# Retention layer and top-2 mixture of experts on one core: the first expert's w1 loaded and cast later, its low products last, other turn halves

## The chip, the cores and the metric

The kernel runs on one core of a Trainium2 chip. The metric is the device time of one execution in microseconds, the median of the runs shown. A profiled execution gives the trace; its span is the time from the first to the last instruction that the profiler saw.

## What is computed

```python
state = zeros(B, H, D, D)                       # B, H, S, D = 4, 8, 768, 64
for t in range(S):
    state = gamma[h] * state + outer(k[:, :, t], v[:, :, t])
    y[:, :, t] = q[:, :, t] @ state / sqrt(D)
x = y as [3072 tokens, 512]
noisy = x @ w_gate + log1p(exp(x @ w_noise)) * noise     # 8 experts
top2, weights = the two largest of noisy, softmax over the two
for e in range(8):                              # w1[e] 512 x 1024, w2[e] 1024 x 512
    out[tokens of e] += weight * (relu(x[tokens of e] @ w1[e]) @ w2[e])
```

All inputs and outputs are float32.

## The kernel before

**First part, the steps.** The tokens are 24 chunks of 128 (4 batches of 6). `step(j)` works on chunk j. On TensorE it issues, in this order: the score products of the next chunk (`qk(j + 1)`, L354), the turn of the chunk before (`x_turn(j - 1)`, L405), the product with the running state (`y_state(j)`, L371, not in the first chunk of a batch), the product of the masked scores with the scaled values (`y_mm(j)`, L378), and the state's update (L388, not in the last chunk of a batch). VectorE masks the scores (`am`, L359) and scales the result (`yt`, L382), GpSimd scales the values (`vp`, L335) and makes the low half of x (`x_low`, L437), ScalarE does squares, splits and copies. x goes to memory as two fp16 halves (`x_store`, L448).

**Turns.** `x_turn` transposes y and multiplies by the gate weights at once. For a chunk in the list `HALVES` it issues 8 matmuls of 128 rows of y; for a chunk that is not in the list 16 matmuls of 64 rows (two parts of the same work). So a turn "in halves" is one whose number is not in the list. The turn of chunk j runs in step j + 1. A float32 matmul shows as two in the trace.

**Inputs.** Each chunk has two loads of 512 KB, `in_qk` and `in_vk`, with AHEAD + 1 = 5 buffers. All are issued by SyncE, which takes its instructions in program order. Before the steps chunks 0 to 3 are issued, then `load(j + 4)` in step j.

**Second part, the experts.** Routing by VectorE tables gives each expert a list of token rows. `gather` reads them (GpSimd's indirect DMA), `x_t` transposes them by DMA into `xe`. Weights come in four parts (`w_load`), are squared and summed for a scale (`w_sum`, L210, `w_scale`), cast to an fp16 high part (`w_hi`, L233) and, by VectorE, to a low part `w1l` (`w_lo_half`, L245, half a part at a time). Each product is three matmuls: high x high, high x low, low x high. The first 384 tokens of expert 0 (`first(0)` to `first(7)`, eight units of 12 matmuls, L888 to L890) start while the last chunks' routing is still being worked out; `step(23)` stands in the middle of `first(0)`.

**What sets the order.** The kernel runs under a manual schedule: every engine's order is that of the code. `at(j, f)`, `at0(j, f)` and `P(j, f)` put work at the end of step j, in the order `late`, `mid` (P), `todo` (at), `first_todo` (at0). `own_a`, `own_h` and `own_t` build the tables of expert 0's tokens (`a` of 128 lanes, `ob` of 7 blocks), `own_m` multiplies them, `slots` makes the row indices; `route_e` copies the running counts (`cum`).

## Time and profile before

| | |
|---|---|
| median of 3 runs | 643.73 us (641.87 to 644.48) |
| the profiled execution's own time | 644.79 us |
| its span | 643.0 us |
| TensorE busy | 625.2 us, 97% |
| ScalarE, VectorE, GpSimd busy | 302.7, 291.1, 203.6 us |
| moved by DMA | 113.04 MB |

The profiled execution took 1.06 us more than the median, and its span leaves out 1.8 us of its own time. A view by line or time gives start, duration, engine, source line and operation (output <- inputs); a bracket tells how long the engine had been idle and what it waited for. The end of a matmul is modelled, so the length of a step is read from the starts of its matmuls.

### The profile page before, as it was taken

Reading aid. Unit: us, or ns where it says so; the run is one execution under the profiler, and the core shown is the slowest. Engines: PE = TensorE matmul, PEld = TensorE weight load, DVE = VectorE, ACT = ScalarE, POOL = GpSimd, SP = SyncE. Lnnn points to the kernel's source line nnn. Section 1 sums busy time; section 2 is a strip of 40 time slices with the busy share of each in tenths; the row PEclk is TensorE's granted clock in tenths of the full one; section 3 lists DMA queues with packets and bytes.
Section 4 is the critical chain, followed back from the end, with each engine's and each line's share of the span. In section 5 each row is a group of like instructions: output and inputs, shape, how many; then the busy total and the mean of one; then the engine's idle time right before and its main releaser. Section 6 shows DMA issues by size and latency. Waiting matters only on the chain.

```text
span 643.0 us, 12833 instructions
## 1 busy us (share of the span) xinstructions
PE 625.2 (97%) x5223; PEld 379.2 (59%) x5223; DVE 291.1 (45%) x736; ACT 302.7 (47%) x582; POOL 203.6 (32%) x169
## 2 busy tenths in 40 slices
PE   8998989999999999999999999999999999999995
PEld 5887877559578545554455445544554465455574
DVE  4667997997454221654262226222622262215020
ACT  5778557615652443554354344434543454344121
POOL 2555556032540143104320533043303420430214
PEclk9999999999999999999999999999999999999998
DMA  8999997998769067736673567557744764472303
GB/s 304 407 407 407 325 368 139 335 243 294 163 106 303 10 123 131 234 84 110 123 212 131 102 130 199 143 88 129 202 151 84 134 197 148 91 140 35 49 9 44
DMA packets 87656, 113.04 MB, mean 176 GB/s; under 512 B 59910, under 2 KB 61068, under 8 KB 84012
## 3 DMA queue, kind: packets, MB, share of 16 engines
q1 hardware_dynamic: 75808, 85.56, 43.4%
q0 software_dynamic: 11776, 26.63, 22.5%
q8 instruction: 42, 0.69, 0.4%
q14 instruction: 18, 0.15, 0.1%
q10 hardware_dynamic: 12, 0.01, 0.0%
HBM read 72.66 MB, written 26.42 MB: 154 GB/s over the span
## 4 chain that ended last, share of the span: by engine, by line
PE 90%; DVE 3%; DMA 2%; issue 2%; POOL 1%; ACT 1%; SPq 0%; POOLq 0%; ACTq 0%; DVEq 0%
PE pH L888 13%; PE pH L890 13%; PE pH L889 13%; PE pO L934 12%; PE pO L936 12%; PE pO L935 12%; PE pY L378 3%; PE pA L354 3%; PE pT L405 2%; PE pT L990 2%; PE pO L978 2%; PE pY L371 1%; DMA xbuf<-x 1%; PE pU L388 1%; DMA in_vk<-vk 1%
## 5 line engine op out<-in xcount | busy, mean ns | idle before, releaser
L925 POOL DMA_INDIRECT out<-ot,idx x51 | 84.4, 1654 | 320.4 <-ACT ot L920 191.7
L888 PE MATMUL pH<-xe,w1h 128*128 128x384 f16 (+5 forms) x576 | 180.9, 314 | 1.1 <-DVE ga L539 1.1
L890 PE MATMUL pH<-xe,w1l 128*128 128x384 f16 (+5 forms) x576 | 180.9, 314 | 0.0
L889 PE MATMUL pH<-xe,w1h 128*128 128x384 f16 (+5 forms) x576 | 180.8, 314 | 0.0
L897 DVE SCALAR_TENSOR_TENSOR hl<-pH,hh 128x384 f16<-128x384 f32 (+5 forms) x144 | 75.6, 527 | 140.1 <-ACT hh L894 139.4
L936 PE MATMUL pO<-w2h,hl 128*128 128x512 f16 x344 | 130.4, 379 | 0.0
L935 PE MATMUL pO<-w2l,hh 128*128 128x512 f16 x344 | 130.4, 379 | 0.0
L934 PE MATMUL pO<-w2h,hh 128*128 128x512 f16 x344 | 130.4, 379 | 0.0
L894 ACT ACTIVATE hh<-pH 128x384 f16<-128x384 f32 (+5 forms) x144 | 67.1, 467 | 122.9 <-PE pH L890 112.0
L920 ACT ACTIVATE ot<-pO,gse 128x512 f32<-128x512 f32 x45 | 30.9, 687 | 155.2 <-PE pO L936 142.9
L238 DVE SCALAR_TENSOR_TENSOR w1l<-wst,wsc,w1h 128x1024 f16<-128x1024 f32 x28 | 35.9, 1283 | 97.6 <-ACT w1h L233 97.6
L888 PEld LDWEIGHTS <-w1h 128*128 128x128 f16 x576 | 56.3, 98 | 34.2 <-issue 3.9
L890 PEld LDWEIGHTS <-w1l 128*128 128x128 f16 x576 | 56.3, 98 | 31.0
L889 PEld LDWEIGHTS <-w1h 128*128 128x128 f16 x576 | 56.3, 98 | 29.7
L210 ACT ACTIVATE junk<-wst 128x1024 bf16<-128x1024 f32 x64 | 67.2, 1050 | 0.0
L743 POOL DMA_INDIRECT xg<-xbuf,idx x54 | 55.3, 1025 | 29.3 <-issue 12.4
L936 PEld LDWEIGHTS <-hl 128*128 128x128 f16 x344 | 33.6, 98 | 40.6
L934 PEld LDWEIGHTS <-hh 128*128 128x128 f16 x344 | 33.6, 98 | 40.6 <-issue 0.4
L935 PEld LDWEIGHTS <-hh 128*128 128x128 f16 x344 | 33.6, 98 | 39.6
L437 POOL TENSOR_TENSOR x<-x,x 128x512 f16<-128x512 f32 x23 | 27.4, 1190 | 41.2 <-ACT x L436 19.3
L233 ACT ACTIVATE w2h<-wst,wsc 128x1024 f16<-128x1024 f32 x32 | 36.5, 1139 | 0.8 <-DVE wsc L188 0.8
L233 ACT ACTIVATE w1h<-wst,wsc 128x1024 f16<-128x1024 f32 x32 | 36.2, 1137 | 0.0
(185 smaller groups left out, 660.0 us busy)
## 6 DMA issues: line engine op xcount, KB each, us to landing
wst<-w SPq DMA_DIRECT2D x28, 1024.0 KB, 7.8
in_qk<-qk SPq DMA_DIRECT2D x24, 512.0 KB, 7.9
in_vk<-vk SPq DMA_DIRECT2D x23, 512.0 KB, 8.7
xbuf<-x SPq DMA_DIRECT2D x24, 256.0 KB, 7.2
out<-zero SPq DMA_DIRECT2D x6, 1024.0 KB, 8.8
wst<-w SPq DMA_DIRECT2D x8, 512.0 KB, 7.4
xg<-xbuf,idx POOLq DMA_INDIRECT x54, 4.7
xe<-xg SPq DMA_TRANSPOSE x54, 4.5
```

What stands on the lines that cost most here:

```text
L210: nc.scalar.activation(junk, st[:, i * 1024:(i + 1) * 1024], AF.Square, accum_out=ss[:, i:i + 1])
L233: nc.scalar.activation(hi, st[:, i * 1024:(i + 1) * 1024], AF.Copy, scale=sc[:, 0:1])
L743: nc.gpsimd.indirect_dma_start(out=x[:n], out_offset=None, in_=xbuf[:128 + B0 * S] if e == 0 and t < 3 else xbuf, in_offset=bass.IndirectO ...
L888: nc.tensor.matmul(p[:, :n], whi, xh, start=(k == 0), stop=False)
L889: nc.tensor.matmul(p[:, :n], whi, xl, start=False, stop=False)
L890: nc.tensor.matmul(p[:, :n], wlo, xh, start=False, stop=(k == KT - 1))
L894: nc.scalar.activation(hh[:, f, n0:n1], p, AF.Relu)
L897: nc.vector.scalar_tensor_tensor(hl[:, f, n0:n1], p, 0.0, hh[:, f, n0:n1], op0=OP.max, op1=OP.subtract)
L925: nc.gpsimd.indirect_dma_start(out=out, out_offset=bass.IndirectOffsetOnAxis(ap=idx[:n, i:i + 1], axis=0), in_=ot[:n], in_offset=None, com ...
L934: nc.tensor.matmul(p, a, WT["2h"][:, f, :], start=(f == 0), stop=False)
L935: nc.tensor.matmul(p, a, WT["2l"][:, f, :], start=False, stop=False)
L936: nc.tensor.matmul(p, c, WT["2h"][:, f, :], start=False, stop=(f == FT - 1))
```

## The change

The loads of w1's four parts for expert 0 move from steps 2 to 5 to steps 5, 7, 9 and 11, their sums to steps 8, 10, 11 and 13, the casts from steps 9 to 12 to steps 14 to 17. w2's loads move from steps 14 to 17 to 16 to 19, its sums from 18, 20, 22 to 20, 22, 23. Seven of the eight low halves of w1 stood in steps (10, 11, 12, 14, 18, 21, 23); four stand there now (17, 21 and two in 23), and the four others between the units of the first tokens. In those units the four low x high matmuls come after the eight others. Inputs are issued three chunks ahead up to step 13, then four; chunks 0 and 1 come in two DMAs for each load. The list of unhalved turns goes from 11 entries (0 to 14 even, 18, 20, 22) to 8. `own_t` goes ahead of `own_h`, all of `own_h` into step 16, `route_e` into step 17; the last routing's `route_p` and `own_m` move about one unit back.

```diff
-HALVES = [*range(0, 16, 2), 18, 20, 22]
+HALVES = [7, 9, 11, 13, 15, 18, 20, 22]
+MORE = 14
...
+    APART = 2
...
-            if n == "vk" and j == 0:
+            if j < APART:
                 for i in range(2):
                     nc.sync.dma_start(t[:, i], src[:, i * DM:(i + 1) * DM])
...
-    for j in range(3, AHEAD):
-        load(j, ("qk",))
-        load(j - 1, ("vk",))
-    load(AHEAD - 1, ("vk",))
+    load(2, ("vk",))
+    todo_in = list(range(3, NCH))
...
-    P(15, own_h, 0, 0, 2)
     at(16, gates_out, 0)
-    P(16, own_h, 0, 2, 12)
     P(16, own_t, 0)
-    P(16, route_e, 0)
+    P(16, own_h, 0, 0, 12)
...
+    P(17, route_e, 0)
...
-        at(2 + i, w_load, 0, "1", i)
+        at((5, 7, 9, 11)[i], w_load, 0, "1", i)
...
-    for i, j in ((0, 10), (2, 11), (4, 12), (6, 14), (1, 18), (3, 21), (5, 23)):
+    for i, j in ((0, 17), (2, 21), (4, 23), (6, 23)):
         P(j, w_lo_half, 0, "1", i)
...
-        if j + AHEAD < NCH:
-            load(j + AHEAD)
+        while todo_in and todo_in[0] <= j + AHEAD - (j < MORE):
+            load(todo_in.pop(0))
...
+        early = e == 0 and n0 == 0
...
-            nc.tensor.matmul(p[:, :n], wlo, xh, start=False, stop=(k == KT - 1))
+            if not early:
+                nc.tensor.matmul(p[:, :n], wlo, xh, start=False, stop=(k == KT - 1))
+        for k in range(KT if early else 0):
+            nc.tensor.matmul(p[:, :n], WT["1l"][:, k, f * 128:(f + 1) * 128], XE[e][:, k, n0:n1], start=False, stop=(k == KT - 1))
...
+    w_lo_half(0, "1", 1)
...
+    w_lo_half(0, "1", 3)
+    h_lo(*p0)
+    w_lo_half(0, "1", 5)
     w_hi(0, "2", 1)
-    h_lo(*p0)
+    p3 = first(3)
```

**SyncE's queue from step 2 on.** `in_qk` and `in_vk` are a chunk's loads, `xbuf<-x` the store of a finished chunk, `wst` a part of w1, `ct` and `nz` constants and noise. Before:

```order
L448 DMA xbuf<-x_305 128x512
L206 DMA wst_389<-w 128x1024
L272 DMA in_qk<-qk 128x1024
L272 DMA in_vk<-vk 128x1024
L448 DMA xbuf<-x_386 128x512
L206 DMA wst_389<-w 128x1024
L870 DMA nz<-noise 128x192
L272 DMA in_qk<-qk 128x1024
L272 DMA in_vk<-vk 128x1024
L448 DMA xbuf<-x_458 128x512
L206 DMA wst_389<-w 128x1024
L870 DMA ct<-ctab 128x433
```

After:

```order
L449 DMA xbuf<-x_312 128x512
L870 DMA ct<-ctab 128x433
L275 DMA in_qk<-qk 128x1024
L275 DMA in_vk<-vk 128x1024
L449 DMA xbuf<-x_393 128x512
L870 DMA nz<-noise 128x192
L275 DMA in_qk<-qk 128x1024
L275 DMA in_vk<-vk 128x1024
L449 DMA xbuf<-x_470 128x512
L275 DMA in_qk<-qk 128x1024
L275 DMA in_vk<-vk 128x1024
L449 DMA xbuf<-x_552 128x512
```

The four parts of w1 are gone from these steps, and a chunk's loads stand behind the store of a chunk that is one later than before.

**VectorE in steps 16 to 18.** From the tables (`a`, `ob`) of step 16 to the masks `am`; before:

```order
L585 TENSOR_TENSOR a_12_1408<-lanes,lf_12_1406 128x1280
L593 TENSOR_TENSOR ob_12_1493<-blks,lf_12_1406 128x84
L595 TENSOR_TENSOR ob_12_1493<-ob_12_1493,tokn 128x84
L566 COPY cum<-pR 128x9
L567 TENSOR_SCALAR cum<-cum 128x1
L359 TENSOR_TENSOR am<-pA,mask 128x512 x2
L425 TENSOR_SCALAR p2m<-xss 128x1
L426 TENSOR_SCALAR xsa<-p2m 128x1
```

After:

```order
L383 TENSOR_TENSOR yt<-pY,gq 128x512
L594 TENSOR_TENSOR ob_12_1507<-blks,lf_12_1430 128x84
L596 TENSOR_TENSOR ob_12_1507<-ob_12_1507,tokn 128x84
L586 TENSOR_TENSOR a_12_1432<-lanes,lf_12_1430 128x1536
L360 TENSOR_TENSOR am<-pA,mask 128x512 x2
L426 TENSOR_SCALAR p2m<-xss 128x1
```

`ob` is made ahead of `a`, `a` is made in one piece, and the copies to `cum` are gone from in front of the masks. Then the end of step 17, where `idx` is the list of rows for the gather; before, with a low half in step 18:

```order
L656 SCALAR_TENSOR_TENSOR idx<-roww 128x3
L359 TENSOR_TENSOR am<-pA,mask 128x512 x2
L425 TENSOR_SCALAR p2m<-xss 128x1
L426 TENSOR_SCALAR xsa<-p2m 128x1
L382 TENSOR_TENSOR yt<-pY,gq 128x512
L245 SCALAR_TENSOR_TENSOR w1l<-wst_389,wsc_391,w1h 128x512
```

After:

```order
L656 SCALAR_TENSOR_TENSOR roww<-acc 128x3
L657 SCALAR_TENSOR_TENSOR idx<-roww 128x3
L567 COPY cum<-pR 128x9
L568 TENSOR_SCALAR cum<-cum 128x1
L246 SCALAR_TENSOR_TENSOR w1l<-wst_623,wsc_625,w1h 128x512
L360 TENSOR_TENSOR am<-pA,mask 128x512 x2
```

The copies to `cum` and a low half `w1l` now stand between the list and the masks.

**TensorE in the first unit of the expert, behind step 23.** `pH` is the unit's sum, `xe` the gathered tokens. Before, from the end of `y_mm(23)` on:

```order
L378 MATMUL pY<-am,vp 64x128 x8
L888 LDWEIGHTS w1h
L888 MATMUL pH<-xe,w1h 128x384
L889 LDWEIGHTS w1h
L889 MATMUL pH<-xe,w1h 128x384
L890 LDWEIGHTS w1l
L890 MATMUL pH<-xe,w1l 128x384
L888 LDWEIGHTS w1h
L888 MATMUL pH<-xe,w1h 128x384
L889 LDWEIGHTS w1h
L889 MATMUL pH<-xe,w1h 128x384
L890 LDWEIGHTS w1l
```

After, the last rows of the same unit:

```order
L889 LDWEIGHTS w1h
L889 MATMUL pH<-xe,w1h 128x384
L890 LDWEIGHTS w1h
L890 MATMUL pH<-xe,w1h 128x384
L894 LDWEIGHTS w1l
L894 MATMUL pH<-xe,w1l 128x384
L894 LDWEIGHTS w1l
L894 MATMUL pH<-xe,w1l 128x384
L894 LDWEIGHTS w1l
L894 MATMUL pH<-xe,w1l 128x384
L894 LDWEIGHTS w1l
L894 MATMUL pH<-xe,w1l 128x384
```

All four matmuls with `w1l` stand at the end, behind `y_mm(23)`; two of them stood ahead of step 23.

## Rows read from the trace of the kernel before

**Rows 1.** The page: engines' busy us (share) x instructions; instruction queue (packets, MB).

```profile
PE 625.2 (97%) x5223; PEld 379.2 (59%) x5223; DVE 291.1 (45%) x736; ACT 302.7 (47%) x582; POOL 203.6 (32%) x169
...
q8 instruction: 42, 0.69, 0.4%
```

**Rows 2.** Stretches: engines' busy us (x instructions), TensorE's granted clock, DMA share, GB/s.

```profile
4.00:6.00 2.00, 1.94 (x19) 1.08 (x18) 0.42 (x3) 2.00 (x8) 0.00 (x0) 1.00 0.85 180
...
28.00:65.00 37.00, 34.71 (x711) 30.40 (x709) 25.91 (x79) 28.71 (x68) 19.88 (x18) 1.00 1.03 405
...
143.00:643.00 500.00, 492.88 (x2991) 277.01 (x2986) 181.45 (x384) 216.69 (x373) 140.19 (x103) 1.00 0.58 132
```

**Rows 3.** Instructions in order of time: the start, first steps, first "issue" wait.

```profile
2.87 0.91 SPq L270 DMA_DIRECT2D in_vk<-vk  x2
...
8.32 1.16 PE L354 MATMUL pA<-in_qk 64*128 64x128 f32 x16 [1.65 <-DMA in_qk<-qk]
...
10.14 1.09 PE L378 MATMUL pY<-am,vp 128*64 128x128 f32 x16 [0.66 <-POOL vp L335]
...
11.63 1.16 PE L354 MATMUL pA<-in_qk 64*128 64x128 f32 x16
...
15.66 1.16 PE L354 MATMUL pA<-in_qk 64*128 64x128 f32 x16
...
18.29 0.33 SPq L448 DMA_DIRECT2D xbuf<-x  x1
...
19.39 1.16 PE L354 MATMUL pA<-in_qk 64*128 64x128 f32 x16
...
30.08 0.43 PE L371 MATMUL pY<-in_qk,U 64*64 64x128 f32 x2 [0.32 <-issue]
```

**Rows 4.** TensorE's waits, 20 to 107 us: total us, times, longest.

```profile
PE pY L371 <- issue: 2.0, 3, 1.1
...
PE pT L405 <- issue: 1.1, 1, 1.1
```

**Rows 5.** DMA from 9 to 65 us: instruction queue (packets, MB, share); issues with us to landing.

```profile
q8 instruction: 8, 0.13, 1.0%
...
in_qk<-qk SPq DMA_DIRECT2D x15, 512.0 KB, 8.1
```

**Rows 6.** In order of time, steps 16 to 18, and the same `ob` later with GpSimd idle.

```profile
77.31 1.75 PE L354 MATMUL pA<-in_qk 64*128 64x128 f32 x16
...
80.02 1.19 DVE L593 TENSOR_TENSOR ob<-blks,lf 128x84 f16<-128x84 f16 x1
...
83.13 1.75 PE L354 MATMUL pA<-in_qk 64*128 64x128 f32 x16
...
124.07 0.23 DVE L593 TENSOR_TENSOR ob<-blks,lf 128x84 f16<-128x84 f16 x1
```

**Rows 7.** In order of time, steps 18 to 22: a low half beside GpSimd, and TensorE's waits.

```profile
87.29 3.39 DVE L245 SCALAR_TENSOR_TENSOR w1l<-wst,wsc,w1h 128x512 f16<-128x512 f32 x1
...
92.05 1.75 PE L354 MATMUL pA<-in_qk 64*128 64x128 f32 x16 [0.93 <-DVE am L359]
...
94.92 0.78 PE L405 MATMUL pT<-turn,yt 64*64 64x80 f32 x32 [1.11 <-ACT x L431]
```

**Rows 8.** In order of time, the first units of the expert around step 23.

```profile
106.73 0.32 PE L888 MATMUL pH<-xe,w1h 128*128 128x384 f16 x1 [1.07 <-DVE ga L539]
...
110.48 0.34 PE L888 MATMUL pH<-xe,w1h 128*128 128x384 f16 x1
...
111.21 0.74 DVE L245 SCALAR_TENSOR_TENSOR w1l<-wst,wsc,w1h 128x512 f16<-128x512 f32 x1
...
111.56 0.78 PE L405 MATMUL pT<-turn,yt 64*64 64x80 f32 x32
...
111.61 1.35 POOL L437 TENSOR_TENSOR x<-x,x 128x512 f16<-128x512 f32 x1 [2.63 <-ACT x L436]
...
117.79 0.18 PE L512 MATMUL pR<-mb,trib 128*128 128x54 bf16 x1 [0.44 <-DVE mb L501]
```

More of the change, by code (lines that the diff above doesn't have):

```diff
@@ L1047, in moe_kernel @@
     h_hi(*p2)
-    p3 = first(3, lambda: route_p(2))
     route_c(2)
+    w_lo_half(0, "1", 3)
+    h_lo(*p0)
+    w_lo_half(0, "1", 5)
     w_hi(0, "2", 1)
-    h_lo(*p0)
+    p3 = first(3)
     w_lo_half(0, "1", 7)
@@ L1056, in moe_kernel @@
     w_hi(0, "2", 2)
+    p4 = first(4, lambda: route_p(2))
     route_n(2)
+    h_lo(*p3)
     route_d(2)
-    h_lo(*p3)
+    own_a("12")
     route_g(2)
@@ L1063, in moe_kernel @@
         zero_out(i)
-    own_a("12")
-    p4 = first(4)
     h_hi(*p4)
@@ L1070, in moe_kernel @@
     own_t("12")
-    w_lo_half(0, "2", 0)
     p5 = first(5)
@@ L1075, in moe_kernel @@
     h_lo(*p5)
-    w_lo_half(0, "2", 1)
+    w_lo_half(0, "2", 0)
     p6 = first(6)
     h_hi(*p6)
-    own_m("12", 0, NC)
     h_lo(*p6)
+    w_lo_half(0, "2", 1)
     flush()
     out_scale(0, 0, 3)
-    p7 = first(7, lambda: own_m("12", NC, 2 * NC))
+    p7 = first(7, lambda: own_m("12", 0, NC))
+    own_m("12", NC, 2 * NC)
     own_s("12")
```

20 lines of the change are left out of this document (10 added, 10 removed).

## The prediction

> **What bounds the kernel now.** I read the page first, then the stretches, then TensorE's and SyncE's instructions in order of time. TensorE is busy 625.2 of 643.0 us [rows 1]. From 143 us on it works 492.88 of 500 us, and nothing in the diff touches that part [rows 2]; I take it as unchanged. TensorE's clock is granted at 1.00, its 2.4 GHz level, in every stretch, so the clock is no term. What can move is the first 127 us: 24 steps and the first eight units of expert 0. There TensorE is both the longest engine and the one that waits. From 28 to 65 us DMA is at its limit: share 1.03, 405 GB/s [rows 2].
>
> A step's length is read from the starts of its score products. The step from 11.63 to 15.66, with a turn of eight matmuls, took 4.03 us; the next, to 19.39, with the turn in halves, took 3.73 [rows 3]. So the halved turn is the faster one, by 0.30 us, although it has twice the matmuls. The mean is 3.88 us. Many steps are longer, and the reader is to see three kinds of excess: TensorE waits for nothing that the profile names ("issue", four waits of together 3.1 us, the longest 1.1) [rows 4]; it waits on VectorE [rows 6, 7]; it waits at the start, for the first inputs [rows 3].
>
> The "issue" waits I read as waits for instructions. The page has 42 packets of 16 KB on the instruction queue and 10,446 instructions of TensorE, matmuls and weight loads [rows 1], so about one packet for 250 instructions. From 9 to 65 us eight of them passed, in a DMA system that was full [rows 5]. That is an inference from counts.
>
> **The change part by part.** Start: TensorE idles 1.65 us for chunk 1's `in_qk` and 0.66 for chunk 0's scaled values [rows 3], 2.31 in all, which is the most that splitting these loads can give. From 4 to 6 us DMA moved only 180 GB/s at a share of 0.85 [rows 2], so room is there. Against it, two more issues stand ahead of the values' load, and two issues took 0.91 us [rows 3]: a loss of 0.9 at worst. I take the middle, **+0.7**. The Trainium skill's DMA: Bandwidth & Descriptors, section Bandwidth, says to batch transfers to 1 MiB or more, which speaks against the split. No row here compares the two sizes under the same load; by that rule the term would be the loss of 0.9, and the sum 1.6 us worse.
>
> Turns: three fewer entries in the list, three more turns in halves, 3 x 0.30 = **+0.9**. In steps 1 to 7 it is four turns, 1.2 us earlier; 0.3 is given back by step 16. Bounds 0, if inputs or instructions set the pace, and 1.2.
>
> Waits for instructions: before, three parts of w1 were queued by step 4, ahead of chunk 9's load. They go to steps 5 to 11, so the queue is lighter in steps 2 to 4, and as full as before in 5 to 13. I expect half of the 3.1 us back, **+1.5**; above 3.1 nothing is to be had, below see the second rival.
>
> Steps 16 to 18: `ob` took 1.19 us where the same operation takes 0.23 later with GpSimd idle [rows 6]. It ran into GpSimd's work. In the new order it comes ahead of the long `a`, and the `cum` copies leave, so the masks of step 17 can start up to 2 us earlier (two such operations, 0.96 each). TensorE's step from 77.31 to 83.13 took 5.82 us, 2.1 over a halved one; up to 1.1 of it is an "issue" wait, counted above, and the score products after it took 1.75 instead of 1.16 [rows 3, 6]. So 1.0 + 0.6 = 1.6 at most, 0 if `ob` is held again. I take **+1.2**.
>
> Steps 18 to 20: the low half at 87.29 took 3.39 us [rows 7], another 0.74 [rows 8]. Its 2.65 us came out again on TensorE: 0.93 idle, 0.59 in the longer score products, 1.11 on ScalarE, together 2.63 [rows 7]. This half leaves step 18, but one now stands at the end of step 17, ahead of the masks, and GpSimd's subtraction and gather follow there. Even odds that it is held: half, **+1.3**, between 0 and 2.6. For the other halves that leave the steps I count nothing: VectorE is busy 25.9 of 37 us from 28 to 65 [rows 2], and the masks have room.
>
> First unit: TensorE waits 1.07 us at 106.73 [rows 8]. The wait is put down to VectorE's `ga`; the unit also needs the transposed tokens, the end of a chain from step 17's list through gathers and DMA. If that chain starts earlier, it may go. I take half, **+0.5**, between 0 and 1.07.
>
> Low products last: before, `x_turn(23)` stood at 111.56, behind six matmuls from 110.48 on, 0.18 each [rows 8]. Now eight stand there and two fewer ahead of step 23. But two low halves are made by VectorE behind `yt` of step 23. Before, the low half there began at 111.21; the next VectorE work can follow after about 0.65 (estimated from its 0.74, as a start overlaps the end before). Two end at 111.21 + 2 x 0.65 = 112.51, 2.03 after 110.48, plus one matmul 2.21; against 1.08 before, less the 0.36 that left the front: TensorE loses 0.77. GpSimd's subtraction of 1.35 us lies there too [rows 8]; if it holds the second half, the loss is 2.1; I add a quarter of 1.35. Later, `route_p` comes a unit later, so the 0.44 us at 117.79 goes. Together **-0.7**, between -2.1 and -0.3. Three more low halves, 0.74 each, go to VectorE between the units; the later `route_p` and `own_m` cover them with one unit of 12 matmuls, 2.2 us. Without that cover up to 2.2 us would be lost at `own_m`.
>
> ScalarE's casts and sums are the same work in later steps. It is busy 28.7 of 37 us from 28 to 65 [rows 2], and that idle time hides them; without it a cast or sum before the turn's squares would cost its own time of about a us. GpSimd's order is unchanged. Inputs three ahead: a load now stands behind a store, priced as a rival.
>
> Sum: 0.7 + 0.9 + 1.5 + 1.2 + 1.3 + 0.5 - 0.7 = 5.4 us. Against the profiled execution's 644.79 us that is 639.4; it was 1.06 us above the median of 643.73, against which it is 638.3. I take 639.0, between them.
>
> **The rivals.**
>
> *Inputs come late: slower.* Chunk 6's load stands behind chunk 0's store, which came 2.63 us into step 2 (18.29 after 15.66) [rows 3]. Its products are due at the start of step 5, three steps of 3.88 after the start of step 2: 9.0 us remain. A load landed after 8.1 us in the full queue [rows 5]. Each us over 9.0 costs a third of a us in each of the 11 steps for chunks 6 to 16. At 11 us that is 7.3, and the 1.5 on instructions is lost too: 647.8 us. It decides from 9.0 on. Against it: the queue should be shorter, since loads enter later and w1 is spread. Chance 0.08.
>
> *Instructions set the pace of halved turns: no change.* A halved step has 192 instructions of TensorE (96 matmuls, 96 weight loads), the other 160; at 250 a packet that is one packet in 4.9 us instead of 5.5 for alternating steps. Steps 1 to 7 now run seven halved turns in a row, some five packets. At 1.06 us each, the size of the worst waits, 5.3 us are lost and the 1.5 not gained: 645.8. For it: steps 2 and 4 had halves and DMA was as full as later. Against it: the first of the four waits came at 30 us [rows 3], not earlier. Chance 0.12.
>
> *VectorE and GpSimd collide again:* the terms of steps 16 to 18, 18 to 20 and the first unit, 3.0 us, are nothing: 642.0. An operation that is held once is held elsewhere once all shifts. Chance 0.18.
>
> *The "issue" waits have nothing to do with DMA:* 1.5 us are not gained, 640.5. The Trainium skill's Runtime: NRT & Kernel Launch, section Instruction fetch mechanics, says that code is refilled in 16 KiB blocks of 256 instructions and that this is mostly hidden. The packet size agrees with the rows; "hidden" would leave the waits of 1.1 us unexplained. Chance 0.10.
>
> **How the numbers follow.** The forecast, 636 to 641, has 0.52. A measurement of this kernel can tell about 0.5%, 3.2 us, from no change: faster is below 640.5. Faster takes the forecast, half of the last rival and a fifth of the collisions: 0.61. Slower, above 646.9, takes the late inputs and a little of the second rival: 0.10. The rest, 0.29, is no change. The range 635.0 to 644.0 leaves out late inputs, most of the second rival and a better start than I dare to count, together about 0.2.
>
> **What would show it.** Right: steps 1 to 7 at 3.73 us; fewer "issue" waits before 40 us; `ob` near 0.25 us; score products at the start of steps 18 and 20 at 1.16. A wait of about a us on `w1l` in the first unit. Wrong: waits of TensorE for `in_qk` in steps 5 to 15; "issue" waits in steps 2 to 7; a low half of 2 to 3 us at step 17 or 23; a wait at `own_m`.

## The result, and the profile after

The changed kernel took **651.04 us**, the median of four runs (649.42 to 654.51), against 642.8 for the kernel before in the same session: ratio **1.0133**, 95% interval 1.0084 to 1.0182. The forecast was 639.0. It is slower, by more than any case that I priced. All ratios here set the executions of a kernel against those of the kernel before on the same chip; they are close to the quotient of the mean times, and not that of the medians (651.04 to 642.8 would be 1.0128). One execution, of 650.94 us in the last run on the changed kernel, counts as a slow one and is left out of its ratio.

The page of the changed kernel, engines and instruction queue as in [rows 1]:

```profile
PE 627.0 (97%) x5271; PEld 380.7 (59%) x5271; DVE 287.8 (44%) x735; ACT 303.5 (47%) x582; POOL 204.7 (32%) x169
...
q8 instruction: 42, 0.69, 0.4%
```

Its stretches, with the columns of [rows 2]:

```profile
9.00:28.00 19.00, 17.73 (x414) 16.14 (x416) 11.33 (x30) 10.67 (x31) 9.61 (x9) 0.91 0.91 334
28.00:65.00 37.00, 33.44 (x762) 29.95 (x758) 24.42 (x74) 24.82 (x63) 19.46 (x18) 1.00 1.00 378
12.00:14.00 2.00, 2.00 (x20) 1.79 (x16) 0.18 (x1) 0.38 (x1) 1.12 (x2) 0.50 1.01 410
110.00:112.00 2.00, 2.00 (x31) 1.52 (x28) 0.31 (x2) 0.80 (x3) 0.34 (x2) 0.58 0.23 25
```

From 28 to 65 us TensorE is busy 33.44 us, where it was 34.71 [rows 2]. DMA moves 378 GB/s instead of 405, and from 9 to 28 us 334 instead of 412 (the kernel before, same view); eight other profiles with the moved loads, below, have 367 to 385 there, so part of the 334 is this execution's. The two short stretches show what the kernel before did not have before its end: a granted clock of 0.50 and 0.58, the 1.2 GHz level or a mix of both. The page's slices hide it (9 of 10 nearly everywhere); it has to be asked for.

TensorE's waits, 20 to 107 us (as [rows 4]), then 107 to 135:

```profile
PE pY L379 <- issue: 3.1, 2, 1.6
PE pA L355 <- issue: 1.7, 2, 1.3
...
PE pR L515 <- issue: 0.6, 1, 0.6
...
PE pH L889 <- DVE ga L540: 1.6, 1, 1.6
PE pH L889 <- DVE hl L901: 1.0, 1, 1.0
PE pH L894 <- DVE w1l L246: 0.7, 2, 0.4
```

The waits for nothing named are 6.2 us in all from 20 to 107 us, against 3.19 in the kernel before (the 3.1 of [rows 4] and one of 0.18). The order of time tells where they and the low clock lie. All rows are of TensorE, but for one each of VectorE, GpSimd and SyncE:

```profile
10.27 1.09 PE L379 MATMUL pY<-am,vp 128*64 128x128 f32 x16 [1.93 <-POOL vp L336]
...
12.08 2.08 PE L355 MATMUL pA<-in_qk 64*128 64x128 f32 x16
...
35.77 0.44 PE L379 MATMUL pY<-am,vp 128*64 128x128 f32 x4 [1.62 <-issue]
...
42.55 0.60 PE L355 MATMUL pA<-in_qk 64*128 64x128 f32 x5 [1.29 <-issue]
...
79.56 1.34 PE L355 MATMUL pA<-in_qk 64*128 64x128 f32 x16
...
80.40 0.27 DVE L594 TENSOR_TENSOR ob<-blks,lf 128x84 f16<-128x84 f16 x1
...
94.62 0.98 POOL L744 DMA_INDIRECT xg<-xbuf,idx  x1
...
96.04 1.16 PE L355 MATMUL pA<-in_qk 64*128 64x128 f32 x16
...
103.48 2.67 SPq L762 DMA_TRANSPOSE xe<-xg  x1
...
106.03 0.49 PE L379 MATMUL pY<-am,vp 128*64 128x128 f32 x5 [1.53 <-issue]
...
108.73 0.32 PE L889 MATMUL pH<-xe,w1h 128*128 128x384 f16 x1 [1.64 <-DVE ga L540]
...
110.67 1.13 PE L372 MATMUL pY<-in_qk,U 64*64 64x128 f32 x16
111.73 1.97 PE L379 MATMUL pY<-am,vp 128*64 128x128 f32 x16
...
123.94 0.32 PE L889 MATMUL pH<-xe,w1h 128*128 128x384 f16 x1 [1.05 <-DVE hl L901]
```

Read against [rows 3, 6, 7, 8]. Step 1 starts 0.45 us later (12.08), and its score products take 2.08 instead of 1.16, at the low clock behind a wait of 1.93. Two waits of 1.62 and 1.29 us come in steps 6 and 8, in the row of seven halved turns (steps 1 to 7) and right behind it. Step 17 starts 2.25 us late (79.56). Then the forecast gains do come: `ob` takes 0.27 instead of 1.19, and step 21 starts at 96.04, 1.5 us *earlier* than before (97.56 in the trace of before). Then they are lost: the first unit starts at 108.73, 2.0 later than 106.73; the products with the state and with the values behind it take 1.13 and 1.97 us, at the low clock, where the same ones took 0.67 and 1.09 before; the fifth unit waits 1.05 for `hl`, the low half of the hidden values. The second expert product starts 5.1 us late (132.43 against 127.31), the end is 5.7 us late.

### The profile page after: what moved, and what is told of

It reads as the page before. It is cut to its first block, busy times and chain, and to the rows that moved or that the text cites. A ratio compares the mean times of both kernels' runs of the same rounds, so it can differ in the third digit from the quotient of the medians.

```text
span 648.7 us, 12928 instructions
## 1 busy us (share of the span) xinstructions
PE 627.0 (97%) x5271; PEld 380.7 (59%) x5271; DVE 287.8 (44%) x735; ACT 303.5 (47%) x582; POOL 204.7 (32%) x169
## 4 chain that ended last, share of the span: by engine, by line
PE 87%; DVE 7%; DMA 2%; issue 2%; POOL 1%; SPq 1%; ACT 0%; POOLq 0%; DVEq 0%; ACTq 0%
PE pH L889 13%; PE pH L890 12%; PE pH L892 12%; PE pO L938 11%; PE pO L939 11%; PE pO L940 11%; PE pA L355 3%; PE pY L379 3%; PE pT L406 3%; PE pT L994 2%; PE pY L372 1%; DMA in_qk<-qk 1%; PE pU L389 1%; DMA in_vk<-vk 1%; DVE w2l L246 1%
## 5 line engine op out<-in xcount | busy, mean ns | idle before, releaser
L892 PE MATMUL pH<-xe,w1l 128*128 128x400 f16 (+5 forms) x544 | 170.4, 313 | 0.0
L892 PEld LDWEIGHTS <-w1l 128*128 128x128 f16 x544 | 53.2, 98 | 28.9
```

What stands on the lines that cost most here:

```text
L892: nc.tensor.matmul(p[:, :n], wlo, xh, start=False, stop=(k == KT - 1))
```

## Theories

Each experiment below says which of these it tests.

- **T1**: a step with a halved turn has more instructions (192 against 160 of TensorE), and their refills don't keep pace. The new list costs time.
- **T2**: the loss is the work behind step 22: late `w1l`, late `hl`.
- **T3**: the split start costs: late values, a wait, a low clock.
- **T4**, formed after the first four runs: the first unit waits for the gathered tokens, whatever TensorE won in the steps, and the wait is followed by a low clock.
- **T5**: the moved loads cost by themselves. **T7** supposes how: they keep the DMA queues full when the tokens are gathered and transposed.
- **T6**: some of the rows that I took gains from are those of one execution.

In the table "waits" are those of TensorE for nothing named, 9 to 100 us; "tokens" is the time from the third gather's row to the first unit's first product; "ahead" the wait in front of that product; "clock" the sum over stretches of 2 us, from 2 to 140, of 2 us times what the granted clock lacks of 1. One profile each.

| kernel | ratio, interval | waits | tokens | ahead | clock |
|---|---|---|---|---|---|
| before | | 3.19 | 9.6 | 1.07 | 0 |
| before, second profile | | 4.69 | 8.9 | 0.30 | 0 |
| before, no halves | 1.0020, 1.0005 to 1.0035 | 0 | 9.3 | 0 | 0 |
| before, new list | 1.0091, 1.0066 to 1.0117 | 5.30 | 10.4 | 1.81 | 0 |
| before, split start | 1.0028, 1.0016 to 1.0040 | 5.86 | 10.6 | 1.12 | 1.7 |
| before, loads moved | 1.0100, 1.0077 to 1.0123 | 3.48 | 12.1 | 1.49 | 1.7 |
| before, tail | 1.0036, 1.0015 to 1.0057 | 3.33 | 10.3 | 0.56 | 0 |
| before, steps 16 to 18 | 1.0007, 0.9987 to 1.0026 | 2.38 | 11.9 | 1.75 | 0 |
| changed | 1.0133, 1.0084 to 1.0182 | 4.77 | 14.1 | 1.64 | 3.4 |
| changed, old list | 1.0104, 1.0081 to 1.0127 | 3.81 | 13.2 | 4.15 | 3.4 |
| changed, no halves | 1.0087, 1.0059 to 1.0115 | 1.50 | 14.8 | 4.49 | 3.4 |

## Experiments on the changed kernel

**Old list of halved turns.** (The expectation has the parity the wrong way round: steps 2, 4, 6 ... are halved.)

```diff
-HALVES = [7, 9, 11, 13, 15, 18, 20, 22]
+HALVES = [*range(0, 16, 2), 18, 20, 22]
```

> The changed kernel with the old list of halved turns (steps 1, 3, 5, ... halved up to 16); all else as changed. Theory T1 (the refills of TensorE's instructions do not keep pace with the run of halved turns, so two waits of 1.62 and 1.29 us came in steps 6 and 8): the waits for nothing named in steps 6 to 8 go or shrink below 1 us in sum, the score products of step 9 start 1.5 to 3 us earlier than the changed kernel's 46.02, and the whole is 1.5 to 3 us shorter than the changed kernel, ratio to the kernel before about 1.008 to 1.011. Theory T2 (the loss sits behind step 22: late transposes, lower clock, low halves late): step 9 at 45 to 46 and the first unit's first product at the changed kernel's 108.7 or at most 1 us earlier; end within 1 us of the changed kernel. Theory T3 (the split of the first loads): no change either.

Measured 649.06 us, 1.0104. Step 9 starts at 42.09, not 46.02. Of these 3.9 us 2.3 lie ahead of step 2 (14.70 against 17.01), where the profiled execution of the changed kernel had its wait and low clock and this one had neither; from step 2 to step 9 it took 27.4 us against 29.0, which is 1.6 us for T1. But the first unit, in order of time, and two later products:

```profile
106.01 0.48 PE L889 MATMUL pH<-xe,w1h 128*128 128x384 f16 x1 [4.15 <-issue]
...
109.31 1.13 PE L372 MATMUL pY<-in_qk,U 64*64 64x128 f32 x16
110.37 1.97 PE L379 MATMUL pY<-am,vp 128*64 128x128 f32 x16
```

Step 22 starts 3.3 us earlier than in the changed kernel (97.78), the first unit only 2.7, after a wait of 4.15 us, and the clock is at 0.51, 0.50, 0.50 and 0.78 in the stretches from 106 to 114. The span ends 1.3 us earlier: most of what the steps won is gone there, in the wait and the clock behind it. That gave T4. The profile names nothing for this wait; in the next run the same place reads 3.14 us "DMA xe<-xg", the transposed tokens. What ties it to the tokens is the order of time: in all 14 profiles with no other work put ahead of the first unit, its first product comes 2.5 to 4.1 us behind the end of the third transpose's issue, whatever the wait is put down to.

**Start as before**: only chunk 0's `in_vk` is split.

```diff
-            if j < APART:
+            if n == "vk" and j == 0:
```

> The changed kernel with only chunk 0's vk load in two parts, as before; all else as changed. T3 (two more issues ahead of the values' load make vp late, TensorE idles 1.93 us at 10 us and then runs at a granted clock of 0.5 for the score products of step 1): the idle time at 10 us falls to about 0.7, the clock stays at 1.00 between 10 and 16 us, the score products of step 1 take 1.16 instead of 2.08, step 2 starts at about 15.7 instead of 17.01, and the whole is 1 to 1.4 us shorter, if later waits don't eat it. T1 and T2: steps 2 to 5 start earlier, but step 9 or the first unit start where they did within 0.5 us, since another wait takes the place.

Measured 654.69 us, 1.0170 (1.0142 to 1.0197). The start looks as expected: step 2 at 15.10 instead of 17.01, no low clock before 66 us. But the next run keeps the split and has step 2 at 15.17, and none of the other profiles with the split start has a low clock there; so the late start belongs to the one profiled execution of the changed kernel. The time is no better: waits of 1.58 at 66.3, 3.45 at 107.3 and 3.14 at 111.5 go with 6.8 us of lost clock. T3 is not shown, neither for the start nor for the loss.

**w2's loads back in steps 14 to 17.**

```diff
-        at(16 + i, w_load, 0, "2", i)
+        at(14 + i, w_load, 0, "2", i)
```

> The changed kernel with the four loads of w2 back in steps 14 to 17 (changed: 16 to 19); all else as changed. T2 (these loads stand beside the gathered tokens' transposes, whose issues took 2.7 to 3.2 us instead of 1.2 to 1.7, so the first unit starts late and the clock falls to 0.57 behind the wait): the issues of the transposes go back to 1.2 to 1.8 us, the wait of 1.64 us ahead of the first unit's first product falls below 0.7, the clock stays at 1.00 from 108 to 116 us, and the whole is 2 to 3 us shorter than the changed kernel. T1: the transposes' issue may change, but the first unit starts at 108 to 108.7 and the whole is within 1 us of the changed kernel. If the transposes stay as slow, the w2 loads are not their cause.

Measured 652.40 us, 1.0140. The transposes took 1.63, 1.23 and 2.00 us to issue, nearly as expected, and yet the third stood at 103.39, as in the changed kernel (103.48), the clock fell to 0.50 from 108 us on, and the tokens took 13.9 us. T2 in this form is refuted: w2's loads alone are not what makes the tokens late.

**Filler ahead of the first unit**, with the old list: twelve matmuls whose result is not used.

```diff
+    busy(12)
     p0 = first(0, lambda: step(j))
```

> The changed kernel with the old list of halved turns, and twelve matmuls of 128x512 on constants (result unused) between the last products of step 22 and the first unit. New theory T4: steps 16 to 22 did get faster, but the first unit waits for the gathered tokens, whose third transpose does not come earlier with TensorE; the wait of 4.15 us there (without the fill) is followed by 8 us at a granted clock of 0.5, which costs 4.4 us more. T4 expects: the first unit's first product stays at 106.0 us within 1 us, the clock stays at 1.00 from 106 to 114 us, the products from 109 to 112.3 take 0.67 and 1.09 us instead of 1.13 and 1.97, and the whole is 3 to 4.4 us shorter than without the fill, ratio 1.003 to 1.006. Rival T1 (instructions of TensorE come late): 24 more instructions make it later, and the clock has nothing to do with the wait: the same ratio as without the fill, 1.010, or above.

In order of time:

```profile
105.31 2.79 PE L126 MATMUL pA<-const-bfloat16-1.0 128*128 128x512 bf16 x11
108.97 0.32 PE L889 MATMUL pH<-xe,w1h 128*128 128x384 f16 x1 [0.86 <-issue]
...
110.76 0.67 PE L372 MATMUL pY<-in_qk,U 64*64 64x128 f32 x16
111.36 1.09 PE L379 MATMUL pY<-am,vp 128*64 128x128 f32 x16
```

The clock stays at 1.00, and the products take 0.67 and 1.09 as forecast. But 648.61 us, 1.0093, is a miss: 3 to 4.4 us were expected, and by the ratios 0.7 came. From the first unit to the end of the span it gained 2.1 us (539.3 against 541.4), less than the 3.4 of clock, since products that come sooner wait 1.6 us for `w1l` (0.3 without the filler). And this execution came to the first unit 3.0 us later than 106.01, with 6.5 us of waits before 100 us against 3.8, although the two programs are alike up to there.

**Work instead of filler**: the turn and the products of the last chunks ahead of all of the first unit's products, with the old list.

```diff
-            if k == 2 and between:
+            if k == (0 if e == f == 0 else 2) and between:
```

> The changed kernel with the old list of halved turns, and the turn and the products of chunks 22 and 23 (3.7 us of work at full clock) ahead of all of the first unit's products instead of behind the first four. T4: this work fills the wait of 4.15 us, the first unit starts 0 to 1.5 us behind it without a fall of the clock, and the turn of chunk 23 starts at 108 to 109.5 instead of 114.76; whole 5 to 6 us shorter than without it, ratio 1.000 to 1.003. T2 (low halves and the wait for hl set the rest): the same start, but at least 2 us are waited out again behind it for w1l or hl: ratio 1.004 to 1.007. T1: the wait named for nothing moves to the first unit as it stands, ratio near 1.010.

Measured 645.55 us, 1.0045 (1.0025 to 1.0064): 3.5 us less than with the old list alone (3.8 by the ratios), in the range set for T2, short of the 5 to 6 us set for T4. No low clock, and waits of 0.89 for VectorE and 0.43 for ScalarE ahead of the unit; then 1.13 for `w1l` and 1.04 for `hl`.

**No turn in halves.**

```diff
-HALVES = [7, 9, 11, 13, 15, 18, 20, 22]
+HALVES = list(range(NCH))
```

> The changed kernel with no turn in halves. T1 (the seven halved turns in a row outrun the refills of TensorE's instructions): the waits for nothing named before 100 us, 4.8 us in the changed kernel, go as they went in the kernel before without halves; the whole is 3 to 5 us shorter than the changed kernel, ratio 1.005 to 1.008. Rival T5 (the moved loads and casts cost most by themselves, whatever the turns): at most 2 us shorter, ratio 1.010 or above. Either way what is left above 1.000 is to be found behind step 16.

Measured 648.84 us, 1.0087, between the two expectations. Before 98 us waits of 0.55 and 0.15 are left (T1); one of 0.80 stands at 98.87, at a routing product, and the two next kernels without halves have one of 1.36 and 1.55 there, so not every wait for nothing named goes with the halves. GpSimd's third gather, SyncE's third transpose and TensorE's first product, in order of time:

```profile
90.31 0.98 POOL L744 DMA_INDIRECT xg<-xbuf,idx  x1 [0.15 <-issue]
...
98.64 2.42 SPq L762 DMA_TRANSPOSE xe<-xg  x1
...
105.15 0.48 PE L889 MATMUL pH<-xe,w1h 128*128 128x384 f16 x1 [4.49 <-issue]
```

The third gather and the third transpose of the kernel before:

```profile
97.10 0.98 POOL L743 DMA_INDIRECT xg<-xbuf,idx  x1
...
102.08 1.23 SPq L761 DMA_TRANSPOSE xe<-xg  x1
```

The gather starts 6.8 us earlier than in the kernel before, the first unit 1.6 earlier than 106.73 (and 1.0 later than in the second profile of before). The tokens took 14.8 us from there, 9.6 in the kernel before.

**No halves, and the work ahead of the first unit.**

```diff
-HALVES = [7, 9, 11, 13, 15, 18, 20, 22]
+HALVES = list(range(NCH))
...
-            if k == 2 and between:
+            if k == (0 if e == f == 0 else 2) and between:
```

> The changed kernel with no turn in halves, and the turn and products of the last two chunks ahead of all of the first unit's products. Without the second edit TensorE waited 4.49 us ahead of the first unit, and then ran 8 us at a clock of about 0.5 (4.4 us). T7 (the loads that were moved to a later time keep DMA full when the gathered tokens are due, so these come about 4 us later after their gathers than in the kernel before; wait and clock are what is lost): 3.7 us of work fill the wait, the clock stays at 1.00, the turn of chunk 23 starts at 107.5 to 109, the whole is 5 to 6.5 us shorter than without the edit, ratio 0.999 to 1.002. Rival T2 (low halves and the wait for hl lose the rest): at most 4 us shorter, ratio 1.003 or above.

```profile
101.73 1.12 PE L406 MATMUL pT<-turn,yt 64*128 64x80 f32 x16 [0.43 <-ACT x L432]
...
105.70 0.34 PE L889 MATMUL pH<-xe,w1h 128*128 128x384 f16 x1 [1.23 <-DMA xe<-xg]
...
107.76 1.12 PE L406 MATMUL pT<-turn,yt 64*128 64x80 f32 x16
```

**642.11 us, 0.9991 (0.9979 to 1.0004)**: 6.7 us less by the medians, 6.2 by the ratios, as T7 expected (5 to 6.5). The wait left, 1.23 us, is now put down to the transposed tokens, the clock stays at 1.00, and the turn of chunk 23 starts at 107.76. By the ratios the halves are worth 0.5% (with intervals that overlap) and the wait ahead of the first unit with its clock 1.0%; the two edits together take all of the loss away. The clock is not that of one profile: the mean granted clock over the whole span is on record for each execution, 0.996 to 0.998 in all twelve here, 0.988 to 0.995 in the six without the second edit and in the four of the changed kernel. `hl` still costs 1.02 there.

**No halves, and the loads of the kernel before**, four chunks ahead.

```diff
-MORE = 14
+MORE = 0
...
-        at((5, 7, 9, 11)[i], w_load, 0, "1", i)
-        at0((8, 10, 11, 13)[i], w_sum, 0, "1", i)
-        at0(14 + i, w_hi, 0, "1", i)
-        at(16 + i, w_load, 0, "2", i)
+        at(2 + i, w_load, 0, "1", i)
+        at0(5 + i, w_sum, 0, "1", i)
+        at0(9 + i, w_hi, 0, "1", i)
+        at(14 + i, w_load, 0, "2", i)
...
-    for i, j in ((0, 17), (2, 21), (4, 23), (6, 23)):
+    for i, j in ((0, 10), (2, 11), (4, 12), (6, 14)):
```

> The changed kernel with no turn in halves, and w1, w2 and the inputs loaded and cast in the steps of the kernel before, four chunks ahead throughout; the four low halves in steps 10 to 14. The split start, steps 16 to 18, and the part behind step 22 stay as changed. T7: DMA moves 400 GB/s or more from 9 to 65 us again, against 384 to 389; the third gather to the first unit takes 9 to 12 us instead of 14.8, the wait ahead of the first unit falls below 1.8 us, the clock stays at 1.00, the whole is 4 to 5.5 us shorter than with the moved loads, ratio 1.000 to 1.003. Rival (the first unit comes late by the split start or by the tail): the wait stays above 3 us, and the ratio at 1.006 or more.

The same three places as in the kernel without halves:

```profile
90.96 0.98 POOL L746 DMA_INDIRECT xg<-xbuf,idx  x1
...
97.70 1.79 SPq L764 DMA_TRANSPOSE xe<-xg  x1
...
102.09 0.32 PE L891 MATMUL pH<-xe,w1h 128*128 128x384 f16 x1
```

The profile goes as T7 says: tokens in 11.1 us, no wait ahead of the unit, clock at 1.00, DMA at 408 and 407 GB/s from 9 to 65 us. The time does so only in some executions: the twelve lie between 641.25 and 650.94, median 646.41, ratio 1.0041 (1.0015 to 1.0068), 2.4 us less than without the edit (3.0 by the ratios), where 4 to 5.5 were expected. The profiled one took 641.99. The longer ones lose clock: the mean granted clock is 0.998 in the four shortest (up to 643.47) and 0.991 to 0.993 in the six from 645.54 to 648.36, and 0.007 of 645 us is 4.5 us, most of the difference. Behind which wait it falls there was not seen.

## Experiments on the kernel before

**The new list alone.**

```diff
-HALVES = [*range(0, 16, 2), 18, 20, 22]
+HALVES = [7, 9, 11, 13, 15, 18, 20, 22]
```

> The kernel before with the new list of halved turns alone (steps 1 to 7 and every second later step). T1 (TensorE's instructions don't keep pace with seven halved turns in a row): two waits for nothing named of 1 us or more come before 45 us, step 9 starts at 44 to 46 us instead of 43.04, and the whole is 1 to 3 us longer, ratio 1.002 to 1.005. My prediction's term: step 9 starts 1.2 us earlier, at 41.8, ratio 0.998 to 0.999. T4: what is gained or lost there is half taken up by the wait ahead of the first unit, since the gathered tokens hang on the steps up to 17.

TensorE's waits, 20 to 107 us:

```profile
PE pA L354 <- issue: 2.2, 2, 1.5
...
PE pR L514 <- issue: 1.1, 1, 1.1
PE pY L378 <- issue: 0.7, 1, 0.7
```

**647.89 us, 1.0091**: over five us lost, where T1 had said 1 to 3. Step 9 starts at 45.68, as T1 said. The waits are 5.3 us, against 3.2 and 4.7 in the two profiles of before: T1's waits hold only a part of the loss. Another 1.81 us stand ahead of the first unit, as a wait for the transposed tokens.

**No turn in halves.**

```diff
-HALVES = [*range(0, 16, 2), 18, 20, 22]
+HALVES = list(range(NCH))
```

> The kernel before with no turn in halves (eight matmuls in every turn). T1 (TensorE's instructions set the pace of the steps, so a halved turn saves its 0.30 us only where the instructions keep up): thirteen turns cost 0.30 us more each, 3.9 us, but the waits for nothing named fall from 3.2 us to under 1.5; the whole is 1 to 2.5 us longer than before, ratio 1.001 to 1.004. Rival (the waits don't hang on how many instructions a step has): the waits stay at 3 us, the whole is 4 us longer, 1.006. If instructions cost more than I think, the ratio is below 1.000.

All of TensorE's waits from 20 to 107 us, and (columns as in [rows 2]) the stretch from 28 to 65:

```profile
PE pT L405 <- ACT x L431: 1.1, 1, 1.1
PE pR L602 <- DVE cum L566: 0.7, 1, 0.7
PE pA L354 <- DVE am L359: 0.3, 1, 0.3
```

```profile
28.00:65.00 37.00, 37.00 (x703) 33.80 (x701) 27.91 (x102) 30.59 (x72) 20.40 (x19) 1.00 1.03 407
```

Not one wait for nothing named is left. TensorE is busy 37.00 of 37 us with 703 matmuls, where the kernel before was busy 34.71 with 711, and DMA is as full (1.03) as there [rows 2]. So a full DMA alone does not bring these waits; with halved turns they come. Ratio 1.0020 (1.3 us, 0.3 to 2.2), as T1 expected: the 3.9 us that thirteen whole turns cost come back for the most part.

**The split start alone.**

```diff
-            if n == "vk" and j == 0:
+            if j < 2:
```

> The kernel before with the loads of chunk 1's qk and vk, and chunk 0's qk, in two parts as well. My prediction's term: 0.7 us gained, between 0.9 lost and 2.3 gained; ratio 0.999. T3 (the split delays the first values, and the wait is followed by a low clock): step 2 starts 0.5 to 1.4 us later than 15.66, ratio 1.001 to 1.002. Undoing the split in the changed kernel made it no faster, which speaks for the first.

Measured 643.55 us, 1.0028: 1.0 to 2.6 us lost. In this execution step 2 starts at 14.89, 0.8 *earlier* than 15.66, but the kernel before has 14.95 in its second profile, without the split: a gain of the start is not shown, nor a loss there. The waits are 5.9 us, one of 1.93 at 82.15, with a clock of 0.57 and 0.58 in the two stretches from 82 to 86. Neither expectation fits; where the time goes in the other executions was not seen.

**The tail alone.** Low products last, the low halves 1, 3, 5 and the routing between the units; the other four halves stay in steps 10 to 14.

```diff
-    for i, j in ((0, 10), (2, 11), (4, 12), (6, 14), (1, 18), (3, 21), (5, 23)):
+    for i, j in ((0, 10), (2, 11), (4, 12), (6, 14)):
...
+    w_lo_half(0, "1", 3)
+    h_lo(*p0)
+    w_lo_half(0, "1", 5)
     w_hi(0, "2", 1)
-    h_lo(*p0)
+    p3 = first(3)
```

> The kernel before with the part of the change behind step 22 alone: the low products of the first eight units at the end of each unit, the low halves 1, 3 and 5 made between the units, and the routing of the last group a unit later. The other four low halves stay in steps 10 to 14, so no product waits for them. T2 as it now stands (the low halves that are made late and the order of VectorE's work there cost about 2 us): only the wait for hl ahead of the fifth unit comes, 1.04 us, against the wait of 0.44 for mb that goes, and the low half of 3.39 us leaves step 18, which gains 1 to 2.6 us there; whole 0 to 2 us shorter, ratio 0.997 to 1.000. My prediction's terms for these parts, without the w1l wait: 1.3 gained in step 18, 0.4 gained at the routing; ratio 0.997. If the ratio is above 1.001, the units lose more than the one wait for hl.

The fifth unit, in order of time:

```profile
115.78 0.32 PE L889 MATMUL pH<-xe,w1h 128*128 128x384 f16 x1 [1.04 <-DVE hl L901]
```

Measured 643.29 us, 1.0036 (1.0015 to 1.0057): 1 to 3.7 us lost, where 0 to 2 were to be gained. The one wait of 1.04 comes as expected: the fifth unit takes the first one's PSUM buffer, which `h_lo(*p0)` frees, and that stands behind two low halves now. The rest is not seen in the profile.

**The loads alone**: w1, w2 and inputs as changed (the diff of the run with the loads of the kernel before, the other way round), low halves behind the casts.

```diff
-    for i, j in ((0, 10), (2, 11), (4, 12), (6, 14), (1, 18), (3, 21), (5, 23)):
+    for i, j in ((0, 17), (2, 20), (4, 21), (6, 22), (1, 23)):
...
-    w_lo_half(0, "1", 7)
+    for i in (3, 5, 7):
+        w_lo_half(0, "1", i)
```

> The kernel before with w1 loaded in steps 5 to 11 and cast in 14 to 17, w2 loaded in 16 to 19, and inputs three chunks ahead up to step 13; the low halves follow the casts (four in steps 17 to 22, one in 23, three behind the fourth unit). My prediction's term: the queue is lighter in steps 2 to 4, half of the waits for nothing named go, 1.5 us gained; ratio 0.998, less what the later low halves cost. T5: the loads of w1 beside the inputs make the full stretch no shorter and spread the waits for instructions: the waits stay at 3 us or more, step 14 starts at 65 us or later, w1l is waited for by 0.7 us in the first unit; ratio 1.001 to 1.004.

Measured 647.95 us, **1.0100**, two and a half times T5's most. DMA moves 367 GB/s from 9 to 28 us (412 before), the waits stay at 3.5 us, the tokens take 12.1 us, the clock falls to 0.64 and 0.51 from 84 to 88 us. Waits of 0.62 for a sum of w2, 0.76 for `mb` and 1.03 for `ob` come between the units.

**Steps 16 to 18 alone.**

```diff
-    P(15, own_h, 0, 0, 2)
...
-    P(16, own_h, 0, 2, 12)
     P(16, own_t, 0)
-    P(16, route_e, 0)
+    P(16, own_h, 0, 0, 12)
...
+    P(17, route_e, 0)
...
-    for i, j in ((0, 10), (2, 11), (4, 12), (6, 14), (1, 18), (3, 21), (5, 23)):
+    for i, j in ((0, 10), (2, 11), (4, 12), (6, 14), (1, 17), (3, 21), (5, 23)):
```

> The kernel before with two parts of the change alone: in steps 15 to 17 ob ahead of a and the copies of cum behind the slots, and the low half of w1 that stood in step 18 moved to the end of step 17. Reading of the two traces (from step 17 to step 21 the changed kernel gained 3.75 us): ob takes about 0.25 us instead of 1.19, the low half 0.75 instead of 3.39, step 21 starts 2.5 to 4 us earlier than 97.56, and the whole is 1.5 to 4 us shorter than before, ratio 0.994 to 0.998. Rival: one of the two operations is held by GpSimd elsewhere, or the gained time is waited out again ahead of the first unit for the gathered tokens; then the first unit starts within 1 us of 106.73 and the ratio is 0.999 to 1.001.

VectorE's two operations and TensorE's first unit, in order of time:

```profile
76.22 0.27 DVE L593 TENSOR_TENSOR ob<-blks,lf 128x84 f16<-128x84 f16 x1
...
81.26 0.74 DVE L245 SCALAR_TENSOR_TENSOR w1l<-wst,wsc,w1h 128x512 f16<-128x512 f32 x1
...
102.46 0.32 PE L887 MATMUL pH<-xe,w1h 128*128 128x384 f16 x1 [1.75 <-DMA xe<-xg]
```

Both operations are freed, as expected; `ob` took 1.19 to 1.21 in every profile with the old order that I read and 0.23 to 0.28 in every one with the new. Measured 642.21 us, 1.0007: no gain in the time, the rival's number. 1.75 us stand ahead of the first unit as a wait for tokens (T4). The unit itself does come earlier, 102.46, but this profile is of the shortest of twelve executions (640.88).

**The same, with the work ahead of the first unit**; then also without halves; then with halves from chunk 16 on only.

```diff
-            if k == 2 and between:
+            if k == (0 if e == f == 0 else 2) and between:
...
-HALVES = [*range(0, 16, 2), 18, 20, 22]
+HALVES = list(range(NCH))
...
-HALVES = [*range(0, 16, 2), 18, 20, 22]
+HALVES = [*range(0, 16), 18, 20, 22]
```

> The kernel before with ob ahead of a, the copies of cum later and the low half of step 18 at the end of step 17 (as in the changed kernel), and the turn and products of the last two chunks ahead of all of the first unit's products. T4: the 1.75 us of waiting ahead of the first unit, seen without the second edit, are filled; the turn of chunk 23 starts at 105 to 106 instead of 107.28; whole 1.5 to 2.5 us shorter than without it, ratio 0.996 to 0.998, and the times of single executions scatter less, since no fall of the clock hangs on that wait. Rival: TensorE waits as long for the copy of U or for yt ahead of the turn, and the time stays at 1.000.

> The kernel before with ob ahead of a, the copies of cum later, the low half of step 18 at the end of step 17, the last two chunks' turn and products ahead of the first unit, and no turn in halves. Without halves alone the waits for nothing named were gone and 2.1 us were lost to VectorE at steps 17 to 20 (0.67, 0.34, 1.12 us); the first part of the change takes these away. T1: no wait for nothing named before 100 us, the first unit at 100.5 to 102.5, ratio 0.995 to 0.998. Rival (the time won in the steps is waited out for the gathered tokens again): the first unit at 103 or later, ratio 0.999 to 1.002.

> As the last one, but with turns in halves from chunk 16 on, two of three or more as in the kernel before, and whole ones in chunks 0 to 15, while DMA is at its limit. T1: no wait for nothing named before 65 us; behind it five halved turns give 0.30 us each, 1.5 us, less what waits come; ratio 0.993 to 0.997, 0 to 1.5 us shorter than with no halved turn. Rival (the waits don't hang on a full DMA system but on the halved turns alone): waits of together 1 us or more between 70 and 100 us, and a ratio at or above that without halved turns.

Measured 0.9997 (0.9975 to 1.0018), 0.9986 (0.9958 to 1.0015) and **0.9963 (0.9939 to 0.9987), 639.24 against 643.14 us**. The first misses its expectation by far and has the rival's number, but only 0.43 us of the rival's wait (for `U`). The second misses by a little (0.995 to 0.998), with the first unit at 103.14, as its rival had it; its two longest executions, 646.44 and 646.92, have a mean granted clock of 0.989, where the nine up to 643.14 have 0.996 to 0.998. The last is what T1 expected, and the one version here that beats both kernels. It has no wait for nothing named before 78 us, and then 0.53 and 0.56 where the halves begin, the 1 us of the rival. That the late halves add to the gain is not settled, since the last two intervals overlap.

**The kernel before again**, one execution.

> The kernel before, unchanged, profiled in a second execution. Theory T6 (the rows that I took gains from are partly those of one execution, 644.8 us, above the median of 642.3): waits for nothing named of another size and at other steps, the low half of step 18 held for another time than 3.39 us, the first unit 1 to 3 us earlier than 106.73. Rival: the program runs in order, so the same rows come within 0.2 us, and ob takes 1.19 and the low half 3.39 again.

VectorE's `ob` and low half, and TensorE's first unit, in order of time:

```profile
79.31 1.20 DVE L593 TENSOR_TENSOR ob<-blks,lf 128x84 f16<-128x84 f16 x1
...
86.75 2.10 DVE L245 SCALAR_TENSOR_TENSOR w1l<-wst,wsc,w1h 128x512 f16<-128x512 f32 x1
...
104.14 0.32 PE L888 MATMUL pH<-xe,w1h 128*128 128x384 f16 x1 [0.30 <-DVE yt L382]
```

This execution took 642.38 us, 2.4 less than the profiled one. `ob` repeats (1.20), the low half does not (2.10 against 3.39), nor does the wait of 1.07 ahead of the first unit (0.30, for `yt`), which starts 2.6 us earlier. Its waits for nothing named are 4.7 us against 3.2, and from step 17 to step 21 it took 18.10 us, not 20.25. T6 holds for two of the three rows.

## Why the prediction was wrong

**Two steps failed, and one was missing.**

- *Turns, +0.9.* 0.30 us a turn is right in a step without waits (steps 2 to 4 of the changed kernel took 3.73 us each), but the term's lower bound of 0 was not: the new list alone loses over five us. My second rival had this mechanism, with five waits of 1.06; I gave it 0.12, since the first wait in the trace came at 30 us. The sign that I named, a wait in steps 2 to 7, came: 1.62 us in step 6. The waits hold only a part of that loss, though; the rest is not traced. The kernel without halves shows that the waits hang on the halves and not on the full DMA alone.
- *Waits for instructions, +1.5.* I counted four waits of 3.1 us; the trace has five of 3.19. A lighter queue gave nothing back: with the loads moved alone 3.48 us of waits, against 3.19 and 4.69 in two profiles of before. The moved loads cost 1.0% by themselves.
- *Missing: the tokens' chain.* I read the 1.07 us ahead of the first unit [rows 8] as a small gain, and did not ask what sets its end. From the third gather on it takes 9 to 12 us in all kernels of the table whose loads were not moved, and 12 to 15 in those where they were (17.2 with the start as before). Part of what TensorE wins ahead of it is waited out there, and the clock falls behind the wait: without halves step 22 starts 5.8 us earlier than in the changed kernel, the first unit 3.6, and the span ends 2.0 earlier. Filling the wait with work, in the changed kernel without halves, was worth 6.2 us by the ratios.
- *Why the tokens come late* is not shown. For T7: from 85 to 105 us DMA moves 335 GB/s in the changed kernel and 310 in it without halves, against 299 before, and undoing the loads in the latter brought 310 to 268 GB/s and 14.8 to 11.1 us. Against it: with w2's loads back it was 278 GB/s and still 13.9 us, and between the third gather and the third transpose DMA moved 277 GB/s without halves and 279 with the loads undone as well. The traces show two places where the chain grows. SyncE took 8.9 and 8.5 us to issue the three transposes in the changed kernel and in it without halves, 4.2 before, and 4.7 with the loads undone. With w2's loads back it took 4.9, but waited 8.5 us for gathered rows (6.2 before).
- *Steps 16 to 18 and 18 to 20, +2.5.* The mechanism was right: `ob` took 0.27 us and the low half of step 17 0.74. The size is less sure: from step 17 to 21 the changed kernel took 16.48 us, the two profiles of the kernel before 20.25 and 18.10, so it gained 3.8 or 1.6. Part of that went into the wait above. The rival that VectorE and GpSimd collide again did not come in this profile; with the old list the low half of step 17 took 1.67 us.
- *First unit, +0.5.* Wrong sign: 1.64 instead of 1.07, and 2.0 us later.
- *Start, +0.7.* The split alone loses 1.0 to 2.6 us, beyond my bound of 0.9, although its first steps come no later; where the loss arises is not shown.
- *Low products last, -0.7.* The wait for `w1l` was 0.72, as forecast 0.77. Not forecast was the buffer of the first unit, 1.05 us at the fifth. No wait came at `own_m`.
- *Inputs late*, the rival with the worst time, did not come: 0.5 us for `in_qk` in all.

The Trainium skill's Runtime: NRT & Kernel Launch, section Instruction fetch mechanics, says that the cost of crossing a block of instructions is mostly hidden. The trace agrees for whole turns (no wait at all in 37 us) and differs for halved ones (2.4 to 6.5 us of waits from 9 to 100 us with 13 or 16 halved turns, if these are refills). That they are refills is still an inference: the waits go when the instructions get fewer, and no run showed the refill itself. What also stays open is why the parts, each alone, add up to 2.6% where the whole costs 1.3 (smaller moves, as that of the constants, were not run alone), and what the longer executions of some kernels wait for before they lose clock.

## What to carry to other kernels

Ahead of a stretch that starts with data from a chain (list, gather, transpose), find the chain's end first: time won on the busiest engine before it is in part waited out there, until the wait is filled with work that is due anyway. Loads that are moved to "where they are needed" can cost by themselves (1.0% here); look at what else is due late. And read a gain of a us or two from more than one profile, for waits of that size move from one execution to the next. Where one profile is all there is, the granted clock of the other executions tells whether they share its loss.

## What the runs showed of the hardware

A wait of TensorE can cost twice. Behind the waits of 1.93 us (the start, and at 82 us with the split start) and of 4.15 and 4.49 us ahead of the first unit the granted clock fell to the 1.2 GHz level (0.50 to 0.58) for 4 to 8 us; by the sum of the column "clock" that is 1.7 to 3.4 us on top. In the changed kernel it fell behind waits of 1.53 and 1.64 us with about 1 us of work between them, with the loads moved alone behind 1.12 and 0.34. Behind single waits of 1.62, 1.74 and 1.81 us elsewhere it stayed at 1.00; behind one of 1.58 and one of 1.65, at 66 us, it fell. So the length of one wait did not tell here. The Trainium skill's TensorE: Matmul & The Clock Gate, Part 1, says that the throttled state is the default one and that activity releases it; the trace agrees: 0.50 behind the idle 4.15 us, 1.00 with matmuls in the same place. In the wait itself a few matmuls without use held the clock at 1.00, and work that was due held it as well and gained more (1.0093 and 1.0045, against 1.0104).
